# Capped attention and two feed-forward layers in split f32: a 16-bit low-bits step, new planner costs, and one more pair of weight blocks by seven products

## The chip, the core and the metric

The kernel runs on one core of a Trainium2 chip, in one launch. The metric is the device time of that launch in microseconds; less is better. The kernel before took 559.13 us (median of three runs, 558.51 to 560.42).

## The reference: what is computed

```python
scores = cap * tanh((q @ k.T / sqrt(64)) / cap)   # batch 2, 12 heads, 448 rows, 64 wide
attn   = exp(scores - max) / (sum + 1e-9)
x      = (attn @ v) as (896, 768)                  # heads side by side
h = x @ w_in;   g = s * relu(h)**2 + b;   x = g @ w_out          # layer 0: 768 -> 2048 -> 768
h = x @ w_in2;  g = h * clip(h + 3, 0, 6) / 6;  out = g @ w_out2 # layer 1: 768 -> 2048 -> 768
```

All inputs and the output are f32; 896 rows are two batches of 448.

## The kernel before: how it is built and what sets its order

**Stages.** Attention first (to about 88 us), then 18 early pieces of layer 0 interleaved with the end of attention, then the two layers. Everything is kept transposed: features on the 128 partitions, the 448 rows of one batch along the free axis.

**Split products.** A value of the two layers is held as two tiles, an upper part rounded to TensorE's fast f32 form (fp32r) and the rest ("hi" and "lo"). A *piece* is one 128x128 weight block against one 448-column tile and takes three matmuls (L230: hi x lo, lo x hi, hi x hi). `PIECE` in the planner is one of them.

**Weights.** A weight arrives in the raw tile as eight bytes each, the bits of a 64-bit float, and is turned into f32 on the chip by four steps in `convert` (L467): `rescale` on ScalarE (L211) takes the upper word as f32 and shifts its exponent; `low_bits` on ScalarE (L218) takes three bits from the top of the lower word and writes them beside the upper word; `shift` on VectorE (L222) moves the rescaled bits left by three; `merge` on VectorE (L228) joins both with the sign. `parts` (L485) then makes hi (ScalarE cast, L492) and lo (VectorE subtraction, L494), in a weight tile of pool gA or gB, two of each. Input-side blocks are 768 wide, two to a pair; output-side blocks are 512 wide, two to a group of 1024. Three raw tiles are filled by SyncE's DMA queue (L200), each as soon as the merge of its former content is done.

**Products.** 16 blocks `f` of 128 hidden features make a layer's first half. A pair of blocks by the plain way is 24 pieces (two blocks, two batches, six pieces each). By Strassen and Winograd's way (`strassen`, L614) it is seven products P1 to P7 of three pieces, 21 pieces, and needs more of the other engines: four sums of weight parts (L520 to L523), sums T1 to T4 of the two batches' inputs (L651, once per layer) with their hi and lo (L442, L445), copies of PSUM banks (L619, L622) and sums of them (L626, called d1, before P7 and L629, called d2, before P4). The result of each block and batch goes through ScalarE and VectorE: in layer 0 relu (L576), square (L579), hi (L587), lo (L593). Before the change the first `PLAIN` = 8 blocks of layer 0 are plain, four pairs, and the other twelve pairs of the two layers go by seven products. After each half of the blocks come six output groups of 16 pieces (`out_block`, L530), which read the hi and lo of that half's eight blocks.

**Order.** The instruction order of the two layers is made when the program is built, by `Plan` (L52). Every step is a task with an engine, a cost, its predecessors and the tiles it holds. The planner gives each task a due time from TensorE's sequence, then goes through a simulated time in which each engine takes the task that is due first among those whose predecessors ended at least `LAG` ago; TensorE may choose among its next 36 pieces. The order that comes out is written into the engines' queues, and on the chip each engine keeps to its queue. The costs (L411 to L413) thus change only the order.

Of the kernel before, what the change touches and what calls it, by code (L numbers as in the profile page):

```python
# [7 lines left out]
F32 = mybir.dt.float32  # L8
F32R = mybir.dt.float32r
U32 = mybir.dt.uint32  # L10
U8 = mybir.dt.uint8
I32 = mybir.dt.int32
AF = mybir.ActivationFunctionType
ALU = mybir.AluOpType
PSUM = bass.MemoryType.PSUM

B, H, S, D = 2, 12, 448, 64
# [11 lines left out]
WARM = (S, S, S // 4)  # L29
SCALE = 1.0 / D**0.5  # L30
FIRST = 3
PLAIN = 8
SLOTS_A, SLOTS_B = 36, 48
GROUPS = {"gA": 2, "gB": 2}
OUT_ORDER = (0, 3, 1, 4, 2, 5)
# [16 lines left out]
class Plan:  # L52


    LAG = 0.15
    WINDOW = 36

    def __init__(self, sizes):
# [2 lines left out]
    def add(self, engine, cost, run, after=(), use=(), soon=None):  # L61
        t = Task(engine, cost, run, after, list(use), len(self.tasks))
        for u in t.use:
            u.left += 1
        for a in t.after:
            a.then.append(t)
        t.soon = soon
        self.tasks.append(t)
        return t
# [102 lines left out]
def attention_moe_moe(ctx: ExitStack, tc: tile.TileContext, qk, v, cap, w1i, w1o, s, b, w2i, w2o, out):  # L172
    nc = tc.nc
# [6 lines left out]
    st = const.tile([128, 1], F32, name="st")  # L180
# [24 lines left out]
    def rescale(raw, n, bits, dve=False):  # L205
        up = raw_up(raw, n).bitcast(F32)
        up = up.rearrange("p (n m) -> p n m", m=BL) if len(bits.shape) == 3 else up
        if dve:
            nc.vector.tensor_scalar(bits, up, 2.0**-112, None, op0=ALU.mult)
        else:  # L210
            nc.scalar.activation(bits, up, AF.Copy, scale=2.0**-112)  # L211

    def low_bits(raw, n, dve=False):
        by = raw[:, :n, :].rearrange("p m t -> p (m t)").bitcast(U8).rearrange("p (m t) -> p m t", t=8)
        if dve:
            nc.vector.tensor_scalar(by[:, :, 4], by[:, :, 3], 5, None, op0=ALU.logical_shift_right)
        else:
            nc.scalar.activation(by[:, :, 4], by[:, :, 3], AF.Copy, scale=1.0 / 32.0, bias=-15.5 / 32.0)  # L218

    def shift(bits):  # L220
        bits = bits.bitcast(U32)
# [185 lines left out]
    def feed_forward(sb):  # L407
        banks = first_ps + [psum()] + [ps_v.tile([128, 512], F32, name="pav") for _ in range(3)] + [ps_z.tile([128, 512], F32, name="pz")]
        plan = Plan({"slot": 0, "bank": 0, "raw": 0, "gA": 0, "gB": GROUPS["gB"]})
        add = plan.add  # L410
        dve = lambda n, ps=False: 0.15 + 0.00105 * n + (0.06 if ps else 0)  # L411
        dve2 = lambda n: 0.16 + 0.00051 * n
        acts = lambda n, bias=False: 0.19 + 0.00085 * n + (0.08 if bias else 0)  # L413
        PIECE = 0.609
        pools = {"a": [sa, SLOTS_A], "b": [sb, SLOTS_B]}

# [9 lines left out]
        def t_of(r, dt):  # L426
            if r.tile is None:
                where = next(p for p in pools.values() if p[1] > 0)
                where[1] -= 1
                r.home = where  # L430
                r.tile = where[0].tile([128, S], dt, name="sl", tag="s")
            return r.tile
# [4 lines left out]
        def split(src, after, deadline=None, bias=None, psum_src=False, use_src=()):  # L437

            hi, lo = res("slot"), res("slot")

            def upper():
                nc.scalar.copy(t_of(hi, F32R), src())  # L442

            def lower():
                nc.vector.tensor_sub(t_of(lo, F32R), src(), hi.tile.bitcast(F32))  # L445
            a = add("ACT", acts(S), upper, after, [hi, *use_src], deadline)
            c = add("DVE", dve(S, psum_src), lower, [a], [hi, lo, *use_src], deadline)
            return Value(hi, lo, [a, c])

        held = lambda kind, tile: Res(kind, tile)  # L450
# [16 lines left out]
        def convert(src, n, bits, before, blocks, raw=None, stage=0):  # L467

            r = raw or res("raw")

            def tile_of():
                if r.tile is None:
                    r.tile = raw_tile()
                return r.tile
            f = add("DMA", n * 0.0024, lambda: load_raw(tile_of(), src, n), (), [r]) if raw is None else None
            land = add("WAIT", 0, None, ()) if False else f
            a = add("ACT", acts(n), lambda: rescale(r.tile, n, bits), [land, *before], [r]) if stage < 1 else None
            l = add("ACT", acts(n), lambda: low_bits(r.tile, n), [a, land], [r])
            sh = add("DVE", dve2(n), lambda: shift(bits), [a, *before])
            m = add("DVE", dve(n), lambda: merge(r.tile, n, bits), [sh, l], [r])  # L480
            for k in blocks:
                w_users[k] += [t for t in (a, sh, m) if t is not None]
            return m
# [83 lines left out]
        def activation(layer, f, bi, c_psum, made, c_slot=None):  # L567

            src_res = c_psum or c_slot
            src = (lambda: c_psum.tile[:, :S]) if c_psum else (lambda: c_slot.tile)  # L570
            t = c_slot if (c_slot and layer == 0) else res("slot")
            soon = 1.5 if c_psum else 3.0

            def relu():
                o = t.tile if t is c_slot else t_of(t, F32)
                nc.scalar.activation(o, src(), AF.Relu, **({"bias": three} if layer else {}))  # L576
            a = add("ACT", acts(S, layer), relu, made, [src_res, t] if t is not src_res else [t], soon)
            if layer == 0:
                q = add("DVE", dve(S), lambda: nc.vector.scalar_tensor_tensor(out=t.tile, in0=t.tile, scalar=st, in1=t.tile, op0=ALU.mult, op1=ALU.mult), [a], [t])  # L579
            else:  # L580
                q = add("DVE", dve2(S), lambda: nc.vector.tensor_scalar(t.tile, t.tile, 6.0, 1.0 / 6.0, op0=ALU.min, op1=ALU.mult), [a], [t], soon + 1)
                q = add("DVE", dve(S, True), lambda: nc.vector.tensor_mul(t.tile, src(), t.tile), [q], [t, src_res], soon + 2)
            hi, lo = res("slot"), res("slot")

            def upper():
                if layer == 0:
                    nc.scalar.activation(t_of(hi, F32R), t.tile, AF.Identity, bias=bt)  # L587
                else:
                    nc.scalar.copy(t_of(hi, F32R), t.tile)

            def lower():
                if layer == 0:
                    nc.vector.scalar_tensor_tensor(out=t_of(lo, F32R), in0=t.tile, scalar=bt, in1=hi.tile.bitcast(F32), op0=ALU.add, op1=ALU.subtract)  # L593
                else:
                    nc.vector.tensor_sub(t_of(lo, F32R), t.tile, hi.tile.bitcast(F32))
            h = add("ACT", acts(S, layer == 0), upper, [q], [t, hi])
            l = add("DVE", dve(S), lower, [h], [t, hi, lo])
            G[f, bi] = Value(hi, lo, [h, l])

        G = {}  # L600
# [13 lines left out]
        def strassen(layer, f, w, ops):  # L614

            a, bb, c = new_bank(), new_bank(), new_bank()
            p1 = product(w["A11"], ops["B11"], a)
            head = take_pe()
            cp = add("ACT", acts(S), lambda: nc.scalar.copy(bb.tile[:, :S], a.tile[:, :S]), p1, [a, bb])  # L619
            p5 = product(w["S1"], ops["T1"], c)  # L620
            s5 = res("slot")
            c5 = add("ACT", acts(S), lambda: nc.scalar.copy(t_of(s5, F32), c.tile[:, :S]), p5, [c, s5])  # L622
            p2 = product(w["A12"], ops["B21"], a, [cp], first=False)
            p6 = product(w["S2"], ops["T2"], bb, [cp], first=False, seeded=True)
            mid = take_pe()
            d1 = add("DVE", dve(S, True), lambda: nc.vector.tensor_add(c.tile[:, :S], bb.tile[:, :S], s5.tile), [*p6, c5], [bb, c, s5], 0.5)  # L626
            p7 = product(w["S3"], ops["T3"], bb, [d1], first=False, seeded=True)
            s7 = res("slot")
            d2 = add("DVE", dve(S, True), lambda: nc.vector.tensor_add(t_of(s7, F32), bb.tile[:, :S], s5.tile), [*p7], [bb, s5, s7], 0.5)  # L629
            p3 = product(w["S4"], ops["B22"], c, [d1], first=False)  # L630
            p4 = product(w["A22"], ops["T4"], bb, [d2], first=False, seeded=True)
            tail = take_pe()
            activation(layer, f, 0, a, p2)
            activation(layer, f, 1, c, p3)
            activation(layer, f + 1, 1, None, [d2], s7)
            activation(layer, f + 1, 0, bb, p4)
            return head, mid, tail
# [47 lines left out]
        for layer in range(2):  # L685
            partial = {}
            for half in range(2):
# [5 lines left out]
                for mt in OUT_ORDER:  # L693
# [3 lines left out]
                    for bi in range(B):  # L697
                        before = []
                        if half:
                            p, t = partial[mt, bi]  # L700
                            before = [add("ACT", acts(S), lambda p=p, q=bank[bi]: nc.scalar.copy(q.tile[:, :S], p.tile), [t], [p, bank[bi]])]
                        made.append(product(w, [G[half * HF + k, bi] for k in range(HF)], bank[bi], before, seeded=bool(half)))
                        pe.extend(take_pe())
                    if half == 0:
                        for bi in range(B):
                            p = res("slot")
                            t = add("ACT", acts(S), lambda p=p, q=bank[bi]: nc.scalar.copy(t_of(p, F32), q.tile[:, :S]), made[bi], [p, bank[bi]], 1.0)
# [180 lines left out]
```

## Time and profile before

| | |
|---|---|
| median of three runs | 559.13 us |
| the profiled execution's own time | 558.14 us |
| its span, first to last instruction | 556.4 us |
| TensorE busy | 543.7 us, 98% |
| ScalarE (ACT) busy | 423.6 us, 76% |
| VectorE (DVE) busy | 394.4 us, 71% |
| DMA engines busy | 34% |
| granted TensorE clock | full in every slice of the span |

A matmul's busy time in the profile (about 367 ns) is longer than the distance to the next one, since matmuls are pipelined. So TensorE's pace is read from the distance of starts, and a pause from a start that comes later than that distance. Likewise the next instruction on VectorE or ScalarE starts before the recorded end of the one before.

### The profile page before, as it was taken

What the parts mean: (1) busy time and instruction counts of PE and PEld (TensorE: products, weight loads), DVE (VectorE), ACT (ScalarE), POOL (GpSimd) and SP (SyncE); (2) the same over time, 40 slices, a digit from 0 to 9 for tenths busy, and PEclk for the clock granted to TensorE, in tenths of its full rate; (3) what the DMA queues carried; (4) which work ended last, traced back from release to release, by engine and by line L of the source; (5) the groups of instructions that cost most, each with busy time, mean ns of one, the idle gap of its engine ahead of it and who ended that gap; (6) DMA issues with size and microseconds to landing.
All of it is one profiled execution on the core that took longest, in us unless ns stands there. A gap on an engine that the chain in (4) does not pass through costs nothing.

```text
span 556.4 us, 7002 instructions
## 1 busy us (share of the span) xinstructions
PE 543.7 (98%) x2682; PEld 438.4 (79%) x2682; DVE 394.4 (71%) x587; ACT 423.6 (76%) x549; POOL 0.4 (0%) x5
## 2 busy tenths in 40 slices
PE   8999999999979999999999999999999999999997
PEld 3322234789969998889999999989999888889996
DVE  2689887878988506898866898899554688994400
ACT  6999993399997518899999758985875788888701
POOL 0000000000000000000000000000000000000000
PEclk9999999999999999999999999999999999999999
DMA  8833411042354503222444322212453322125211
GB/s 314 326 107 111 154 53 41 0 152 90 139 151 137 184 1 114 94 77 77 125 147 163 121 107 94 77 65 84 147 197 133 114 94 77 59 98 180 105 51 49
DMA packets 16860, 64.13 MB, mean 115 GB/s; under 512 B 2214, under 2 KB 4154, under 8 KB 16698
## 3 DMA queue, kind: packets, MB, share of 16 engines
q1 hardware_dynamic: 16680, 63.52, 33.8%
q8 instruction: 21, 0.34, 0.2%
q10 hardware_dynamic: 146, 0.16, 0.1%
q14 instruction: 13, 0.11, 0.1%
HBM read 60.88 MB, written 2.79 MB: 114 GB/s over the span
## 4 chain that ended last, share of the span: by engine, by line
PE 71%; ACT 16%; DVE 9%; issue 3%
PE pf L232 31%; PE pav L232 20%; PE pz L232 7%; ACT raw L218 7%; PE ps L265 5%; PE pav L291 4%; ACT w L211 3%; DVE gBl L494 2%; DVE w L228 2%; ACT t L273 2%; ACT gAh L492 1%; PE pav L288 1%; DVE sl L579 1%; ACT t L278 1%; DVE sl L593 1%
## 5 line engine op out<-in xcount | busy, mean ns | idle before, releaser
L232 PE MATMUL pf<-sl,gBh 128*128 128x448 f32 x450 | 128.5, 367 | 0.4 <-DVE sl L593 0.4
L218 ACT ACTIVATE raw<-raw 128x512 uint8<-128x512 uint8 (+1 forms) x77 | 116.9, 1607 | 0.3
L228 DVE SCALAR_TENSOR_TENSOR w<-raw,w 128x512 uint32<-128x512 uint32 (+1 forms) x80 | 63.6, 798 | 46.3 <-ACT raw L218 46.2
L232 PEld LDWEIGHTS pf<-sl,gBh 128*128 128x128 f32 x450 | 84.4, 188 | 8.0 <-DVE sl L593 0.7
L232 PE MATMUL pf<-sl,gBl 128*128 128x448 f32 x225 | 83.0, 369 | 4.9 <-ACT sl L587 2.8
L232 PE MATMUL pav<-sl,gBh 128*128 128x448 f32 x238 | 68.0, 367 | 0.0
L211 ACT ACTIVATE w<-raw 128x512 f32<-128x512 f32 (+1 forms) x79 | 57.9, 763 | 7.6 <-DVE gBl L494 5.4
L232 PE MATMUL pf<-sl,gAh 128*128 128x448 f32 x198 | 56.6, 367 | 0.0
L494 DVE TENSOR_TENSOR gBl<-w,gBh 128x1024 fp32r<-128x1024 f32 (+1 forms) x29 | 37.0, 1277 | 26.5 <-ACT gBh L492 26.4
L232 PEld LDWEIGHTS pf<-sl,gBl 128*128 128x128 f32 x225 | 42.3, 188 | 10.5 <-ACT sl L587 3.1
L232 PE MATMUL pav<-sl,gAh 128*128 128x448 f32 x172 | 49.0, 366 | 0.0
L232 PEld LDWEIGHTS pav<-sl,gBh 128*128 128x128 f32 x238 | 44.7, 188 | 4.0
L222 DVE TENSOR_SCALAR w<-w 128x512 uint32<-128x512 uint32 (+1 forms) x80 | 37.2, 476 | 12.3 <-ACT w L211 11.9
L492 ACT CAST gBh<-w 128x1024 fp32r<-128x1024 f32 (+1 forms) x29 | 31.9, 1100 | 18.3 <-PE pf L232 6.1
L232 PE MATMUL pav<-sl,gBl 128*128 128x448 f32 x119 | 43.8, 368 | 0.0
L273 ACT ACTIVATE t<-ps 128x896 f32<-128x896 f32 x42 | 37.9, 902 | 6.5 <-PE ps L265 6.5
L278 ACT ACTIVATE t<-t 128x896 f32<-128x896 f32 x42 | 39.9, 949 | 1.2
L232 PEld LDWEIGHTS pf<-sl,gAh 128*128 128x128 f32 x198 | 37.2, 188 | 3.4
L494 DVE TENSOR_TENSOR gAl<-w,gAh 128x1536 fp32r<-128x1536 f32 (+2 forms) x24 | 34.3, 1432 | 6.9 <-ACT gAh L492 6.8
L492 ACT CAST gAh<-w 128x1536 fp32r<-128x1536 f32 (+2 forms) x24 | 29.2, 1219 | 13.0 <-DVE w L521 11.4
L232 PE MATMUL pf<-sl,gAl 128*128 128x448 f32 x99 | 36.3, 367 | 0.0
L265 PE MATMUL ps<-rqk 64*128 64x448 f32 x144 | 34.7, 585 | 0.5 <-ACT t L273 0.5
(157 smaller groups left out, 931.4 us busy)
## 6 DMA issues: line engine op xcount, KB each, us to landing
raw<-in_w1i SPq DMA_DIRECT2D x16, 768.0 KB, 4.3
raw<-in_w1o SPq DMA_DIRECT2D x24, 512.0 KB, 3.4
raw<-in_w2i SPq DMA_DIRECT2D x16, 768.0 KB, 4.3
raw<-in_w2o SPq DMA_DIRECT2D x24, 512.0 KB, 3.5
rqk<-in_qk SPq DMA_DIRECT2D x11, 448.0 KB, 5.8
out<-sl SPq DMA_DIRECT2D x12, 224.0 KB, 1.9
rb<-rows SPq DMA_DIRECT2D x10, 224.0 KB, 3.7
va<-in_v SPq DMA_DIRECT2D x1, 1344.0 KB
```

Source lines behind the costliest of these rows:

```text
L211: nc.scalar.activation(bits, up, AF.Copy, scale=2.0**-112)
L218: nc.scalar.activation(by[:, :, 4], by[:, :, 3], AF.Copy, scale=1.0 / 32.0, bias=-15.5 / 32.0)
L222: nc.vector.tensor_scalar(bits, bits, 3, None, op0=ALU.logical_shift_left)
L228: nc.vector.scalar_tensor_tensor(out=bits, in0=up, scalar=0x80000007, in1=bits, op0=ALU.bitwise_and, op1=ALU.bitwise_or)
L232: nc.tensor.matmul(ps[:, :S], w[a], rhs[r], start=start and i == 0, stop=stop and i == 2, skip_group_check=True)
L265: nc.tensor.matmul(ps[:, j, :S], raw_qk[p][rows, 1, c * 128:(c + 1) * 128], raw_qk[p][rows, 0, :], start=True, stop=True)
L273: nc.scalar.activation(u_t[n], u_ps.pop(n)[:, :, :S], AF.Tanh, scale=icap_r)
L278: nc.scalar.activation(u_t[n], u_t[n], AF.Exp, scale=cap_r)
L288: nc.tensor.matmul(pav[p + o][(top, end)[j], :S], va[bi][keys, d, 4 * NC + col, :], u_t[n][keys, col, :], start=o == 1, stop=o == 0)
L291: nc.tensor.matmul(pav[p][(top, end)[j], :S], va[bi][:, d, (2 * (p % 2) + j) * NC + c, :], u_t[n][:, j, :], start=(p % 2 == 0 and c == 0), ...
L492: nc.scalar.copy(g.tile[0][:, at:at + n], cols)
L494: c = add("DVE", dve(n), lambda: nc.vector.tensor_sub(g.tile[1][:, at:at + n], cols, g.tile[0][:, at:at + n].bitcast(F32)), [a], [g])
```

## The change

Three edits. `low_bits` reads and writes the same place through 16-bit instead of 8-bit elements: on ScalarE it multiplies the 16-bit word that holds the wanted bits by 2^-13 where it multiplied the byte by 2^-5. The planner gets other costs and a longer `LAG`. And `PLAIN` goes from 8 to 6, so that the fourth pair of layer 0 (f = 6 and 7) goes by seven products, which puts the T sums of layer 0 before the first group of output pieces and not behind it.

```diff
-PLAIN = 8
+PLAIN = 6
...
-    LAG = 0.15
+    LAG = 0.25
...
     def low_bits(raw, n, dve=False):
-        by = raw[:, :n, :].rearrange("p m t -> p (m t)").bitcast(U8).rearrange("p (m t) -> p m t", t=8)
+        by = raw[:, :n, :].rearrange("p m t -> p (m t)").bitcast(U16).rearrange("p (m t) -> p m t", t=4)
         if dve:
-            nc.vector.tensor_scalar(by[:, :, 4], by[:, :, 3], 5, None, op0=ALU.logical_shift_right)
+            nc.vector.tensor_scalar(by[:, :, 2], by[:, :, 1], 13, None, op0=ALU.logical_shift_right)
         else:
-            nc.scalar.activation(by[:, :, 4], by[:, :, 3], AF.Copy, scale=1.0 / 32.0, bias=-15.5 / 32.0)
+            nc.scalar.activation(by[:, :, 2], by[:, :, 1], AF.Copy, scale=2.0**-13, bias=0.5**14 - 0.5)
...
-        dve = lambda n, ps=False: 0.15 + 0.00105 * n + (0.06 if ps else 0)
-        dve2 = lambda n: 0.16 + 0.00051 * n
-        acts = lambda n, bias=False: 0.19 + 0.00085 * n + (0.08 if bias else 0)
+        dve = lambda n, scalar=False: 0.075 + 0.00104 * n + (0.06 if scalar else 0)
+        dve2 = lambda n: 0.07 + 0.00052 * n
+        acts = lambda n, scaled=False: 0.09 + (0.00093 if scaled else 0.00084) * n + (0.055 if scaled else 0)
...
-            a = add("ACT", acts(n), lambda: rescale(r.tile, n, bits), [land, *before], [r]) if stage < 1 else None
-            l = add("ACT", acts(n), lambda: low_bits(r.tile, n), [a, land], [r])
+            a = add("ACT", acts(n, True), lambda: rescale(r.tile, n, bits), [land, *before], [r]) if stage < 1 else None
+            l = add("ACT", acts(n, True), lambda: low_bits(r.tile, n), [a, land], [r])
```

The other changed lines only say which cost a VectorE step is given.

TensorE, around the fourth pair of layer 0, as it was: the last pieces of block 7 (batch 1, bank pz_830; xh and xl are the hi and lo of the attention's result), then at once the first output group with block 0, 1 and so on (sl tiles), all eight blocks of batch 0 in bank pf_726.

```order
L232 MATMUL pz_830<-xh15_94,gAl_1018 128x448
L232 MATMUL pz_830<-xl15_95,gAh_1017 128x448
L232 MATMUL pz_830<-xh15_94,gAh_1017 128x448
L232 MATMUL pf_726<-sl_920,gBl_1096 128x448
L232 MATMUL pf_726<-sl_936,gBh_1095 128x448
L232 MATMUL pf_726<-sl_920,gBh_1095 128x448
L232 MATMUL pf_726<-sl_926,gBl_1096 128x448
```

The same place now: the last matmul of P1 (bank pav_827), P5 (pav_828), P2 (pav_827), P6 (pav_829), then three output pieces in pz_830, then P7 (pav_829 again, behind d1), P3 and P4.

```order
L232 MATMUL pav_827<-xh02_76,gAh_1037 128x448
L232 MATMUL pav_828<-sl_903,gAl_1038 128x448
...
L232 MATMUL pav_827<-xh03_78,gAl_1038 128x448
...
L232 MATMUL pav_829<-sl_937,gAl_1038 128x448
...
L232 MATMUL pz_830<-sl_1130,gBl_1110 128x448
L232 MATMUL pz_830<-sl_1157,gBh_1109 128x448
...
L232 MATMUL pav_829<-sl_998,gBl_1019 128x448
L232 MATMUL pav_829<-sl_1043,gBh_1018 128x448
...
L232 MATMUL pav_828<-xh13_90,gBl_1019 128x448
...
L232 MATMUL pav_829<-sl_1088,gBl_1019 128x448
L232 MATMUL pav_829<-sl_1115,gBh_1018 128x448
```

24 pieces became 21, and three output pieces stand between P6 and P7.

VectorE, from the end of attention on (behind the last lo of the attention's result), as it was: squares (L579) come between the steps of block 3's weights.

```order
L222 TENSOR_SCALAR w<-w 128x768
L651 TENSOR_TENSOR sl<-xf 128x448
L579 SCALAR_TENSOR_TENSOR sl<-sl,st 128x448 x3
L228 SCALAR_TENSOR_TENSOR w<-raw,w 128x768
L222 TENSOR_SCALAR w<-w 128x768
L228 SCALAR_TENSOR_TENSOR w<-raw,w 128x768
L579 SCALAR_TENSOR_TENSOR sl<-sl,st 128x448
L494 TENSOR_TENSOR gAl<-w,gAh 128x768
```

And now, from the same instruction on: sums of inputs come first, and the first square, which was the second instruction behind that L222, is now the 43rd, behind nearly all the T sums.

```order
L222 TENSOR_SCALAR w<-w 128x768
L651 TENSOR_TENSOR sl<-xf 128x448 x3
L651 TENSOR_TENSOR sl<-xf,sl 128x448
L228 SCALAR_TENSOR_TENSOR w<-raw,w 128x768
L222 TENSOR_SCALAR w<-w 128x768
L651 TENSOR_TENSOR sl<-xf,sl 128x448
L228 SCALAR_TENSOR_TENSOR w<-raw,w 128x768
...
L651 TENSOR_TENSOR sl<-xf,sl 128x448
L445 TENSOR_TENSOR sl<-sl 128x448
L579 SCALAR_TENSOR_TENSOR sl<-sl,st 128x448
L445 TENSOR_TENSOR sl<-sl 128x448
```

Twelve sums and twelve lo parts (L651, L445) thus moved ahead of the 16 squares and 16 lo parts of the first eight blocks' results.

## Rows read from the trace of the kernel before

**Rows 1.** The page: shares of the chain that ended last, by line.
```profile
PE pf L232 31%; PE pav L232 20%; PE pz L232 7%; ACT raw L218 7%; PE ps L265 5%; PE pav L291 4%; ACT w L211 3%; DVE gBl L494 2%; DVE w L228 2%; ACT t L273 2%; ACT gAh L492 1%; PE pav L288 1%; DVE sl L579 1%; ACT t L278 1%; DVE sl L593 1%
```

**Rows 2.** Timeline, TensorE, first output group: start, length, instruction, idle before and releaser.
```profile
153.88 0.36 PE L232 MATMUL pf<-sl,gBl 128*128 128x448 f32 x1
...
157.73 0.57 PE L232 MATMUL pf<-sl,gBh 128*128 128x448 f32 x2
161.05 0.48 PE L232 MATMUL pf<-sl,gBl 128*128 128x448 f32 x1 [2.75 <-ACT sl L587]
161.98 0.67 PE L232 MATMUL pf<-sl,gBh 128*128 128x448 f32 x2 [0.45 <-DVE sl L593]
162.49 0.36 PE L232 MATMUL pf<-sl,gBl 128*128 128x448 f32 x1
```

**Rows 3.** Timeline, TensorE: two other pauses, each behind the matmul before it.
```profile
116.67 0.37 PE L232 MATMUL pav<-xh,gAh 128*128 128x448 f32 x1
117.29 0.47 PE L232 MATMUL pav<-xh,gAl 128*128 128x448 f32 x1 [0.26 <-DVE gAl L494]
...
485.66 0.56 PE L232 MATMUL pf<-sl,gAh 128*128 128x448 f32 x2
487.34 0.47 PE L232 MATMUL pf<-sl,gBl 128*128 128x448 f32 x1 [1.12 <-DVE pz L626]
```

**Rows 4.** Chain of waits in order of time: start, length, merged instructions.
```profile
177.24 14.60 PE pav L232 x72
...
288.63 14.88 PE pav L232 x72
...
537.83 14.89 PE pf L232 x72
```

**Rows 5.** ScalarE by line and form: count, busy us, mean ns, idle before.
```profile
L218 ACT ACTIVATE raw<-raw 128x512 uint8<-128x512 uint8 x48 | 62.1, 1388 | 0.2
L218 ACT ACTIVATE raw<-raw 128x768 uint8<-128x768 uint8 x29 | 54.8, 1971 | 0.1
...
L211 ACT ACTIVATE w<-raw 128x512 f32<-128x512 f32 x48 | 30.9, 672 | 2.0 <-DMA raw<-in_w2o 1.0 <-DMA raw<-in_w1o 0.9
L211 ACT ACTIVATE w<-raw 128x768 f32<-128x768 f32 x31 | 27.0, 905 | 5.5 <-DVE gBl L494 5.4
```

**Rows 6.** Waits, all engines: us in total, times, longest.
```profile
DVE w L228 <- ACT raw L218: 46.2, 61, 3.4
```

**Rows 7.** Timeline, VectorE, behind the attention's end.
```profile
108.17 0.56 DVE L222 TENSOR_SCALAR w<-w 128x768 uint32<-128x768 uint32 x1
...
128.99 0.68 DVE L579 SCALAR_TENSOR_TENSOR sl<-sl,st 128x448 f32<-128x448 f32 x1
129.59 2.46 DVE L593 SCALAR_TENSOR_TENSOR sl<-sl,bt 128x448 fp32r<-128x448 f32 x4
```

**Rows 8.** Timeline, VectorE, before the TensorE pause at 466.5 us.
```profile
463.20 0.96 DVE L228 SCALAR_TENSOR_TENSOR w<-raw,w 128x768 uint32<-128x768 uint32 x1 [1.18 <-ACT raw L218]
464.96 0.96 DVE L228 SCALAR_TENSOR_TENSOR w<-raw,w 128x768 uint32<-128x768 uint32 x1 [0.80 <-ACT raw L218]
465.83 0.62 DVE L629 TENSOR_TENSOR sl<-pf,sl 128x448 f32<-128x448 f32 x1
```

**Rows 9.** VectorE by line and form, as group 5.
```profile
L228 DVE SCALAR_TENSOR_TENSOR w<-raw,w 128x768 uint32<-128x768 uint32 x32 | 30.7, 958 | 24.1 <-ACT raw L218 24.1
L579 DVE SCALAR_TENSOR_TENSOR sl<-sl,st 128x448 f32<-128x448 f32 x32 | 21.3, 680 | 0.2 <-ACT sl L576 0.2
L494 DVE TENSOR_TENSOR gAl<-w,gAh 128x1536 fp32r<-128x1536 f32 x12 | 21.0, 1753 | 2.5 <-ACT gAh L492 2.5
L494 DVE TENSOR_TENSOR gBl<-w,gBh 128x1024 fp32r<-128x1024 f32 x17 | 20.8, 1223 | 6.3 <-ACT gBh L492 6.3
...
L445 DVE TENSOR_TENSOR sl<-sl 128x448 fp32r<-128x448 f32 x24 | 14.7, 620 | 0.3
...
L222 DVE TENSOR_SCALAR w<-w 128x768 uint32<-128x768 uint32 x32 | 17.7, 557 | 7.8 <-ACT w L211 7.8
```

More of the change, by code (lines that the diff above doesn't have):

```diff
@@ L10 @@
 U32 = mybir.dt.uint32
-U8 = mybir.dt.uint8
+U16 = mybir.dt.uint16
 I32 = mybir.dt.int32
@@ L446, in split @@
             a = add("ACT", acts(S), upper, after, [hi, *use_src], deadline)
-            c = add("DVE", dve(S, psum_src), lower, [a], [hi, lo, *use_src], deadline)
+            c = add("DVE", dve(S), lower, [a], [hi, lo, *use_src], deadline)
             return Value(hi, lo, [a, c])
@@ L578, in activation @@
             if layer == 0:
-                q = add("DVE", dve(S), lambda: nc.vector.scalar_tensor_tensor(out=t.tile, in0=t.tile, scalar=st, in1=t.tile, op0=ALU.mult, op1=ALU.mult), [a], [t])
+                q = add("DVE", dve(S, True), lambda: nc.vector.scalar_tensor_tensor(out=t.tile, in0=t.tile, scalar=st, in1=t.tile, op0=ALU.mult, op1=ALU.mult), [a], [t])
             else:
                 q = add("DVE", dve2(S), lambda: nc.vector.tensor_scalar(t.tile, t.tile, 6.0, 1.0 / 6.0, op0=ALU.min, op1=ALU.mult), [a], [t], soon + 1)
-                q = add("DVE", dve(S, True), lambda: nc.vector.tensor_mul(t.tile, src(), t.tile), [q], [t, src_res], soon + 2)
+                q = add("DVE", dve(S), lambda: nc.vector.tensor_mul(t.tile, src(), t.tile), [q], [t, src_res], soon + 2)
             hi, lo = res("slot"), res("slot")
@@ L596, in activation @@
             h = add("ACT", acts(S, layer == 0), upper, [q], [t, hi])
-            l = add("DVE", dve(S), lower, [h], [t, hi, lo])
+            l = add("DVE", dve(S, layer == 0), lower, [h], [t, hi, lo])
             G[f, bi] = Value(hi, lo, [h, l])
@@ L625, in strassen @@
             mid = take_pe()
-            d1 = add("DVE", dve(S, True), lambda: nc.vector.tensor_add(c.tile[:, :S], bb.tile[:, :S], s5.tile), [*p6, c5], [bb, c, s5], 0.5)
+            d1 = add("DVE", dve(S), lambda: nc.vector.tensor_add(c.tile[:, :S], bb.tile[:, :S], s5.tile), [*p6, c5], [bb, c, s5], 0.5)
             p7 = product(w["S3"], ops["T3"], bb, [d1], first=False, seeded=True)
             s7 = res("slot")
-            d2 = add("DVE", dve(S, True), lambda: nc.vector.tensor_add(t_of(s7, F32), bb.tile[:, :S], s5.tile), [*p7], [bb, s5, s7], 0.5)
+            d2 = add("DVE", dve(S), lambda: nc.vector.tensor_add(t_of(s7, F32), bb.tile[:, :S], s5.tile), [*p7], [bb, s5, s7], 0.5)
             p3 = product(w["S4"], ops["B22"], c, [d1], first=False)
```

## The prediction, made before the changed kernel was run

> **What bounds the kernel now.** I first read the page's chain by line: TensorE's matmuls of the two layers (L232) hold 58% of the span, and the one step that stands out beside them is ScalarE's L218, the low bits, with 7%, some 38 us [rows 1]. Then TensorE's timeline from 88 us on, looking for starts that come later than the pace. The pace has two values in this trace, both at full granted clock: 72 matmuls in 14.60 us are 0.2028 us each, 72 in 14.88 us are 0.2067 us [rows 4]. TensorE changes from one to the other at pauses, with no cause that I can see; 242 to 355 us and 487 us to the end run slow, most of the rest fast.
>
> The pauses are few. The largest is in the first output group: two matmuls start at 157.73 and should end their turn at 158.14; the next starts at 161.05, then 161.98, and the two after it take 0.51 instead of 0.41 [rows 2]. Beyond the pace that is 2.91 + 0.73 + 0.10 = 3.7 us, released by ScalarE's L587 and VectorE's L593, the hi and lo of the last plain block. At 117.29 there is one of 0.42 us and 0.11 at its restart, released by L494 [rows 3]. Behind 162 us eight more of 0.2 to 1.4 us each make 4.7 us in all; the last and longest begins behind 485.66 and ends at 487.34, 1.28 us late and 0.11 at the restart, released by L626 [rows 3]. So 9.0 us of pauses could go; the rest of the two layers is TensorE's own work.
>
> Who is late in them is a mixture of ScalarE and VectorE. VectorE waits 46.2 us in 61 places for L218 [rows 6]. Shortly before the pause at 466.5 us its two merges wait 1.18 and 0.80 us for L218, and L629, which TensorE waits for there, stands behind them in the queue [rows 8].
>
> **The nine matmuls.** 24 pieces become 21: 9 matmuls of 0.2028 us, **-1.8 us**, if nothing new makes TensorE wait.
>
> **The 16-bit step.** No row shows a 16-bit operation on ScalarE. The byte form costs 1.97 us for 768 columns and 1.39 for 512; `rescale`, the same function on the same stride of eight bytes in f32, 0.905 and 0.672 [rows 5]. The f32 row is the lower bound that I use, though the step could undercut it a little; the byte rows are the upper, though two bytes could cost more than one. The 16-bit form resembles the byte form in that it writes part of a word in place, and the f32 form in that nothing is narrower than a half word. I take the f32 price, because the byte form's extra is per element (1.07 us over 768, 0.72 over 512, about 1.4 ns each in both), which looks like the handling of a byte operand and not like a fixed cost of writing in place; this is the weakest choice here. By it ScalarE loses 29 x 1.07 + 48 x 0.72 = 65 us of its 424 busy. All but what lies in the pauses is hidden beside TensorE.
>
> The Trainium skill ("ScalarE: Activation LUTs", What ACT_TABLE_LOAD costs) gives one element a cycle at 1.2 GHz for f32 and bf16 alike, 186 ns and 0.833 ns per element. By it a 768-wide step would take 826 ns, an estimate from that page, near the f32 row's 905; the byte row is far from it, and the page says nothing on bytes.
>
> **The first pair by seven products.** In the old trace the first output group starts at 153.88 [rows 2]. The 24 pieces of blocks 6 and 7 before it are 72 x 0.2028 = 14.6 us, so block 6 starts at 139.3. The pause at 117.29 goes: VectorE's L494 stands behind a merge that ScalarE's L218 releases a microsecond sooner. That is **-0.5 us**, and P1 starts at 138.8. P1, P5, P2, P6 and the three output pieces are 15 pieces, 45 matmuls, 9.1 us: TensorE wants P7, and with it d1 (L626), at 147.9.
>
> VectorE has now more to do before d1. Its queue from the L222 at 108.17 [rows 7] holds, up to d1: 5 L222 and 5 L228 of 768, 2 and 2 of 512, 12 L651, 12 L445, lo parts of 768 (three), 1024, 1152 and 1536, four weight sums of 384, 11 squares, 7 lo parts of results, d1. Starts follow at the mean length less 0.08 us (0.60 for the L579 at 128.99, whose mean is 0.680 [rows 7, 9]). So: 5 x 0.48 + 5 x 0.88 = 6.8; the 512-wide ones 2 x 0.34 + 2 x 0.61 = 1.9; L651, L445 and d1, of one size and form of operation, 25 x 0.54 = 13.5; lo parts at 1.14 for 1024, 1.67 for 1536, and by their slope of 1.04 ns per element 1.28 for 1152 and 0.88 for 768, together 6.7; weight sums by the same slope 4 x 0.48 = 1.9; 18 x 0.60 = 10.8 for squares and lo parts, which are also scalar_tensor_tensor of 448. Sum 41.6 us, and about 0.8 us of waits for ScalarE's first merges that are left at the f32 price. d1 is done at 150.6, 2.7 us after TensorE wants it. The copy L619 before P2 stands in ScalarE's queue behind L587s that follow VectorE's squares, so part of these 2.7 us may show one product earlier; the sum is the same.
>
> From there to the last lo that the first group needs it is 10 us more on VectorE, and TensorE has nine pieces of products and seven output pieces, 9.7 us, before it asks for that one: no second pause. So 3.7 us of pause become 2.7: **-1.0 us**. At the byte price each of the five wide merges is held up to 0.9 us longer, and d1 comes some 3.7 us later.
>
> **Later pauses.** Eight, 4.7 us. Before each stand L218 steps of the same pair, two of them worth 2.1 us by rows 5, more than any of these pauses. What does not shorten is VectorE's own work, and two of the longest pauses (2.4 us of the 4.7) are waits for L626 in a queue that is nearly full. I take 1.5 us left, **-3.2 us**, with 0 and 6 as bounds. The planner's new costs and `LAG` act here and nowhere else; they set the order by distances that the rows confirm for VectorE (0.075 + 0.06 + 0.00104 x 448 = 0.60, the L579 distance), and I give them no term of their own.
>
> Attention up to 88 us keeps its order on TensorE; its three low-bits steps on VectorE end nothing there. SyncE's loads keep their order in the weights: each waits for a merge, and the merges come sooner. The tail is the same last product and output.
>
> **Sum.** -1.8 - 0.5 - 1.0 - 3.2 = -6.5 us on the profiled execution's 558.14, that is 551.6 us. The median of the runs before is 1.0 us above that execution, so I predict **552.6 us**. Pace: 188 us of the old trace run at 0.2067. All fast would take off 188 x 2% = 3.6 us more; all slow would add some 5.2 us. I keep the old mixture, and its chance is the largest part of the range. The forecast's own range is 548.5 to 556.5.
>
> **Rivals.**
> *The 16-bit form costs as the byte did (slower).* The Trainium skill ("SBUF — State Buffer", Door 1: The DMA port swizzle) says that an access which crosses into a new 16-byte line pays, so that only a stride of a few elements is free. Here, as a mechanism of this kernel: f32, 16-bit and byte steps all go by eight bytes, the f32 row reads so at 0.9 ns per element [rows 5] and writes packed, so it would be the strided write that costs, and 16 bits leave it. Then the place is d1: 2.7 + 3.7 = 6.4 us of pause instead of 3.7 (+2.7). Further on, both versions of the planner charge L218 less than it costs (0.843 then, 0.859 now), but the old one hid that by charging other ScalarE steps too much: 0.571 for a 448-wide copy that it now charges 0.466. Ten such steps in each of 13 pairs are 13.7 us of allowance gone; the old order was short by 27 us on the 24 wide steps and 36 us on the 48 narrow ones and paid 8.4 us, 13%; so 13% of 13.7, +1.8 us. With -1.8 and nothing else: 558.14 + 2.7 + 1.8 - 1.8 = 560.8, on the median's scale **561.8**. Between -6.5 at 0.905 us and +2.7 at 1.97 the point from which it is slower is about 1.66 us for 768 columns. For it: the partial write. Against it: the per-element extra of the byte.
> *VectorE, not ScalarE, is what is late.* Then the later pauses stay and only the products and the 0.5 us remain, with the first pause as before: 558.14 - 2.3 + 1.0 = **556.8**. For it: two waits are for L626, and VectorE's load in the first stretch. Against it: 46.2 us of VectorE's waits for L218.
> *The pace falls to 0.2067 throughout:* 552.6 + 5.2 = **557.8**. For it: the last 65 us did. Against it: of the pauses most were followed by the fast pace.
>
> **How the numbers follow.** Forecast 0.66, byte price 0.13, VectorE 0.16, slow pace 0.05. A measurement can tell 0.3%, 1.7 us: faster is under 557.45, slower over 560.8. Faster: 0.65 of the forecast, 0.09 of VectorE's case, 0.74 in all; same 0.18, from VectorE's, the pace's and half of the byte's case; slower 0.08, the other part of the byte's. The range is 547.5 to 560: under it lie the fast pace with all pauses gone, over it most of the byte price.
>
> **What would show it.** L218 at 768 columns near 0.9 us and VectorE's wait for it under 20 us in all; nine matmuls fewer; a pause at P7 or P2 near 139 to 151 us of about 2.7 us; no pause in the first output group; behind it few pauses, 1.5 us together; and the share of 0.2067. An L218 above 1.6 us, a first pause over 6 us or more than 5 us of later pauses would make the prediction wrong.

## The result, and the profile after

The changed kernel took 564.43 us (median of six runs, 563.67 to 565.97) against 558.82 us of the kernel before beside it: ratio 1.0102, interval 1.0079 to 1.0125. It is slower by 1%, where 552.6 us and a range of 547.5 to 560 had been forecast. Of e2 below, one execution of six ran at a granted clock of 0.56 from end to end, took 885.09 us and is left out.

The profiled execution took 565.01 us, 6.9 more than that of before. ScalarE by line and form, as [rows 5]:

```profile
L218 ACT ACTIVATE raw<-raw 128x512 uint16<-128x512 uint16 x48 | 62.7, 1383 | 0.1
L218 ACT ACTIVATE raw<-raw 128x768 uint16<-128x768 uint16 x29 | 54.7, 1980 | 0.1
...
L211 ACT ACTIVATE w<-raw 128x512 f32<-128x512 f32 x48 | 31.1, 672 | 4.6 <-DMA raw<-in_w2o 3.2 <-DVE gAl L494 0.9 <-DMA raw<-in_w1o 0.2
L211 ACT ACTIVATE w<-raw 128x768 f32<-128x768 f32 x31 | 27.1, 906 | 4.0 <-DVE gBl L494 2.5 <-DVE gAl L494 1.4
```

The 16-bit form takes 1.980 and 1.383 us where the byte form took 1.971 and 1.388. Nothing was saved. VectorE's wait for it is down only from 46.2 us [rows 6] to 41.5. That wait, and what TensorE waited for in the layers, by line (us in total, times, longest):

```profile
DVE w L228 <- ACT raw L218: 41.5, 52, 1.7
...
PE pav L232 <- ACT pav L619: 6.8, 1, 6.8
PE pz L232 <- DVE sl L629: 1.9, 2, 1.3
PE pav L232 <- DVE pav L626: 1.6, 3, 0.9
```

The 6.8 us are at the fourth pair: P2 waits for the copy L619. TensorE's timeline there, the last two matmuls of P5 first:

```profile
141.63 0.57 PE L232 MATMUL pav<-sl,gAh 128*128 128x448 f32 x2
148.97 0.74 PE L232 MATMUL pav<-xh,gAl 128*128 128x448 f32 x1 [6.77 <-ACT pav L619]
149.51 0.57 PE L232 MATMUL pav<-xl,gAh 128*128 128x448 f32 x1
149.88 0.58 PE L232 MATMUL pav<-xh,gAh 128*128 128x448 f32 x1
...
152.12 0.44 PE L232 MATMUL pav<-xh,gAh 128*128 128x448 f32 x1
152.40 0.37 PE L232 MATMUL pav<-sl,gAl 128*128 128x448 f32 x1
```

P2 should start at 142.04 and starts at 148.97. Its matmuls then follow at 0.37 us, not at 0.20: the granted clock is about half. The next two lines are stretches: from and to, length, then busy time and count of each engine (PE, weight loads, VectorE, ScalarE, POOL), and behind POOL the granted clock:

```profile
148.90:152.50 3.60, 3.53 (x10) 3.17 (x11) 3.40 (x7) 3.36 (x6) 0.00 (x0) 0.53 0.02 5
152.50:160.00 7.50, 7.50 (x38) 6.82 (x37) 7.19 (x14) 4.70 (x8) 0.00 (x0) 1.00 0.00 0
```

0.53 for those 3.6 us, nearly the lower level of 1.2 GHz, then full: some 1.6 us more. What stood before L619 on ScalarE:

```profile
145.04 0.67 ACT L587 ACTIVATE sl<-sl,bt 128x448 fp32r<-128x448 f32 x1 [1.09 <-DVE sl L579]
145.62 0.66 ACT L211 ACTIVATE w<-raw 128x512 f32<-128x512 f32 x1
...
147.16 1.33 ACT L218 ACTIVATE raw<-raw 128x512 uint16<-128x512 uint16 x1
148.23 0.69 ACT L619 COPY pav<-pav 128x448 f32<-128x448 f32 x1
```

P1's last matmul had started at 140.01, so L619's input was there some eight microseconds before it ran. L619 stood behind L587 steps that waited for VectorE's squares, and behind a conversion. The first square (the 45th instruction behind the L222 in this trace, not the 43rd) is late itself: it starts at 140.87, where e1 below, the same order with a cheap step, has it at 136.29. All five wide merges before it waited for L218, 0.39 to 1.06 us each, 3.6 us together:

```profile
117.78 0.96 DVE L228 SCALAR_TENSOR_TENSOR w<-raw,w 128x768 uint32<-128x768 uint32 x1 [1.06 <-ACT raw L218]
...
127.08 0.96 DVE L228 SCALAR_TENSOR_TENSOR w<-raw,w 128x768 uint32<-128x768 uint32 x1 [0.79 <-ACT raw L218]
...
140.87 0.68 DVE L579 SCALAR_TENSOR_TENSOR sl<-sl,st 128x448 f32<-128x448 f32 x1
```

**Where the 6.9 us came from**, by distances of TensorE's starts. The first pair with its restart and the low clock costs 8.5 us, where the first output group had cost 3.7 [rows 2]: +4.8. The pause at 117 is gone: -0.5. Pauses behind the first output group make 9.7 us instead of 4.7: +5.1. Nine matmuls: -1.8. Together +7.6; some 0.5 us less up to the end of attention, and a little less of the slow pace (some 170 us for 184), make up the rest.

### The profile page after: what moved, and what is told of

It reads as the page before. It is cut to its first block, busy times and chain, and to the rows that moved or that the text cites. A ratio compares the mean times of both kernels' runs of the same rounds, so it can differ in the third digit from the quotient of the medians.

```text
span 563.2 us, 7021 instructions
## 1 busy us (share of the span) xinstructions
PE 544.4 (97%) x2673; PEld 437.1 (78%) x2673; DVE 398.1 (71%) x593; ACT 425.0 (75%) x551; POOL 0.4 (0%) x5
## 5 line engine op out<-in xcount | busy, mean ns | idle before, releaser
L218 ACT ACTIVATE raw<-raw 128x512 uint16<-128x512 uint16 (+1 forms) x77 | 117.4, 1608 | 0.1
L232 PE MATMUL pf<-sl,gBh 128*128 128x448 f32 x358 | 102.2, 367 | 0.0
L228 DVE SCALAR_TENSOR_TENSOR w<-raw,w 128x512 uint32<-128x512 uint32 (+1 forms) x80 | 63.5, 797 | 41.9 <-ACT raw L218 41.5
L232 PEld LDWEIGHTS pf<-sl,gBh 128*128 128x128 f32 x358 | 67.3, 188 | 5.9
L232 PE MATMUL pf<-sl,gAh 128*128 128x448 f32 x246 | 70.3, 367 | 0.0
L232 PE MATMUL pav<-sl,gAh 128*128 128x448 f32 x244 | 69.6, 366 | 0.0
L232 PE MATMUL pf<-sl,gBl 128*128 128x448 f32 x179 | 66.0, 369 | 0.7 <-DVE sl L629 0.6
L232 PEld LDWEIGHTS pav<-sl,gAh 128*128 128x128 f32 x244 | 45.9, 188 | 4.0
L494 DVE TENSOR_TENSOR gBl<-w,gBh 128x1152 fp32r<-128x1152 f32 (+1 forms) x26 | 33.5, 1288 | 20.5 <-ACT gBh L492 20.4
L492 ACT CAST gBh<-w 128x1152 fp32r<-128x1152 f32 (+1 forms) x26 | 28.8, 1106 | 24.2 <-DVE w L523 8.7
L222 DVE TENSOR_SCALAR w<-w 128x512 uint32<-128x512 uint32 (+1 forms) x80 | 37.0, 475 | 12.4 <-ACT w L211 11.9
L232 PE MATMUL pav<-sl,gAl 128*128 128x448 f32 x122 | 44.7, 366 | 0.0
```

Of the source, the lines that this page charges most:

```text
L218: nc.scalar.activation(by[:, :, 2], by[:, :, 1], AF.Copy, scale=2.0**-13, bias=0.5**14 - 0.5)
L222: nc.vector.tensor_scalar(bits, bits, 3, None, op0=ALU.logical_shift_left)
L228: nc.vector.scalar_tensor_tensor(out=bits, in0=up, scalar=0x80000007, in1=bits, op0=ALU.bitwise_and, op1=ALU.bitwise_or)
L232: nc.tensor.matmul(ps[:, :S], w[a], rhs[r], start=start and i == 0, stop=stop and i == 2, skip_group_check=True)
L492: nc.scalar.copy(g.tile[0][:, at:at + n], cols)
L494: c = add("DVE", dve(n), lambda: nc.vector.tensor_sub(g.tile[1][:, at:at + n], cols, g.tile[0][:, at:at + n].bitcast(F32)), [a], [g])
```

## The experiments

Each is a small edit of the changed kernel or of the one before; times are medians, ratios are to the kernel before on the same chip.

| | edit | us | ratio, interval |
|---|---|---|---|
| changed kernel | | 564.43 | 1.0102, 1.0079 to 1.0125 |
| e1 | low bits on 3/8 of the columns | 549.89 | 0.9855, 0.9807 to 0.9903 |
| e2 | byte form | 563.68 | 1.0095, 1.0064 to 1.0126 |
| e3 | fourth pair plain | 566.35 | 1.0144, 1.0104 to 1.0183 |
| e4 | true price | 553.72 | 0.9894, 0.9845 to 0.9943 |
| e5 | true price, fourth pair plain | 548.80 | 0.9840, 0.9795 to 0.9885 |
| e6 | before, fourth pair by seven | 557.98 | 0.9989, 0.9963 to 1.0015 |
| e9 | before, true price | 553.18 | 0.9908, 0.9876 to 0.9940 |
| e11 | LAG 0.15 | 566.63 | 1.0161, 1.0111 to 1.0210 |
| e12 | old charges, LAG 0.25 | 556.22 | 0.9977, 0.9951 to 1.0003 |
| v2, seven | whole words | 554.93 | 0.9951, 0.9929 to 0.9973 |
| v2, plain | whole words, fourth pair plain | 552.92 | 0.9918, 0.9889 to 0.9947 |

**e1: the same order with a step that costs what I had assumed.**

```diff
-nc.scalar.activation(by[:, :, 2], by[:, :, 1], AF.Copy, ...)
+nc.scalar.activation(by[:, :n * 3 // 8, 2], by[:, :n * 3 // 8, 1], AF.Copy, ...)
```

> The changed kernel with its own order on every engine, but the low-bits step on ScalarE treats only the first 3/8 of the columns (the other weights keep the rescaled word without their last three bits). The step should then take about 0.88 us at 768 and 0.66 us at 512, the f32 price that I had taken. Theory A (the price of the 16-bit step is what was mis-sized, the rest of the forecast holds): the 6.9 us pause at the first pair by seven products falls to about 2.7 us, time 551 to 555 us. Theory B (VectorE's load and the new order lose the time, whatever the step costs): the pause stays above 5 us, time 560 us or more.

549.89 us. ScalarE's rows, and TensorE's two waits in the layers that are over 0.3 us:

```profile
L218 ACT ACTIVATE raw<-raw 128x192 uint16<-128x192 uint16 x48 | 27.8, 656 | 0.1
L218 ACT ACTIVATE raw<-raw 128x288 uint16<-128x288 uint16 x29 | 23.0, 885 | 0.1
```
```profile
PE pav L232 <- ACT pav L619: 2.1, 1, 2.1
...
PE pav L232 <- DVE pav L626: 0.9, 1, 0.9
```

VectorE's first square there:

```profile
136.29 0.68 DVE L579 SCALAR_TENSOR_TENSOR sl<-sl,st 128x448 f32<-128x448 f32 x1
```

At 0.885 and 0.656 us the pause at the first pair is 2.3 us by distance of starts, at P2 (2.7 forecast, for P7 or P2), the later pauses make 1.9 us (1.5 forecast), and VectorE waits 6.1 us for L218 in all. Two things stand beside that: behind the pause the clock falls and costs 1.6 us, and this execution kept the fast pace, for which the forecast's number is 549. So the time lies under the 551 to 555 us that I expected of e1, in part by the luck of the pace; two of its four executions took 551 to 552. Theory A's mechanism holds, B falls: VectorE's load by itself costs about what the prediction had said.

**e2: the byte form in the new order.**

```diff
-bitcast(U16) ... by[:, :, 2], by[:, :, 1], scale=2.0**-13, bias=0.5**14 - 0.5
+bitcast(U8)  ... by[:, :, 4], by[:, :, 3], scale=1.0 / 32.0, bias=-15.5 / 32.0
```

> The changed kernel with the old byte form of the step and everything else as changed. Theory A (16 bits cost as the byte did): the same time as the changed kernel within 0.3%, 563 to 566 us, L218 at 1.97 and 1.39 us. Theory B (same): no difference. Theory C (the 16-bit form is worth something that the means hide): over 567 us.

563.68 us, the changed kernel's time within the intervals. The two forms are worth the same; that edit does nothing. No row of e2's profile is used.

**e3 and e6: the fourth pair alone.** `PLAIN = 8` in the changed kernel, `PLAIN = 6` in the one before.

> The changed kernel with the fourth pair of layer 0 plain again (24 pieces). Theory A: the order made for a cheap step still loses, but without the pile of work before the first seven products: 558 to 562 us, no pause above 4 us. Theory B: the loss is all in the place of the fourth pair: 556 to 558 us, the old time or less.

> The kernel before with its byte step, costs and LAG, only the fourth pair of layer 0 by seven products. Theory A (the new costs lose the time, the pair gains): 555 to 560 us, nine matmuls fewer against some pause at the first seven products. Theory B (the pair's place loses the time): 562 us or more with a pause above 5 us.

566.35 and 557.98 us. Both theories for e3 missed: the plain pair does not help. It has nine matmuls more, 1.8 us, and its median is 1.9 us above the changed kernel's, though the intervals overlap. The pause is then at the old place and longer (2.75 us in [rows 2]):

```profile
PE pf L232 <- ACT sl L587: 3.9, 1, 3.9
```

In e6 the pair's pause at L619 is 3.4 us, with a stretch of low clock behind it. By distance of starts e6 has 3.6 us more of pauses and low clock than the kernel before; the nine matmuls give 1.8 us back and a larger share of the fast pace the rest: no difference to be measured. So the place of the pair is not the loss, in either order. Nor is it a gain that can be counted on: in the traces of the changed kernel, e1, e4, e6, e11 and e12, whatever the charges, the low clock behind the pause at L619 costs some 1.4 to 1.6 us, nearly all that the nine matmuls save.

**e4, e5, e9: tell the planner the price.**

```diff
-l = add("ACT", acts(n, True), lambda: low_bits(r.tile, n), [a, land], [r])
+l = add("ACT", 0.00227 * n - 0.04, lambda: low_bits(r.tile, n), [a, land], [r])
```

> The changed kernel with the planner told what the step takes by the trace (start to start 1.70 us at 768, 1.12 at 512) and nothing else. Theory A: the planner puts the copy L619 ahead of the conversions that hold it, the 6.9 us pause and the loss of clock behind it go: 553 to 558 us. Theory B: VectorE's work before d1 is the same, so the first pause stays above 4 us and the time above 560 us.

> The changed kernel with the true price of the low-bits step in the planner and the fourth pair of layer 0 plain again. Theory A: the price alone repairs the order; against the run with the price and the fourth pair by seven products this one has nine matmuls more (1.8 us) and no pause at the first L619: 553 to 557 us, under the kernel before. Theory B (the pair's place decides): 557 us or more, or clearly under 552.

> The kernel before with only the price of the low-bits step in its planner set to what the trace shows (1.70 and 1.12 us), its other charges too high as they were. Theory A: the pause of 3.7 us in the first output group goes, later ones shrink: 553 to 557 us. Theory C (the old surcharges had already made up for the price, so that pricing it twice changes little): 557 to 560 us.

553.72, 548.80 and 553.18 us: all three are under the kernel before. e9 is the plainest case: one charge set right in the old kernel, and between 107 and 338 us no start on its TensorE comes late by 0.05 us or more; the 3.7 us of the first output group [rows 2] are gone. In e4 the step still takes 1.988 us at 768, and TensorE waits 2.1 us for L619, with some 1.6 us of low clock behind it, so the loss of clock did not go as I had expected:

```profile
139.30 1.38 ACT L218 ACTIVATE raw<-raw 128x512 uint16<-128x512 uint16 x1
...
142.78 0.54 ACT L576 ACTIVATE sl<-pf 128x448 f32<-128x448 f32 x1 [0.58 <-DVE sl L593]
...
144.15 0.54 ACT L619 COPY pav<-pav 128x448 f32<-128x448 f32 x1
```

The narrow conversions are now done at 140.7; L619 then stands behind other steps of ScalarE, one of which waits 0.58 us for VectorE. e5 is the fastest kernel of the study that computes everything; its largest pause in the layers is 0.7 us:

```profile
PE pav L232 <- DVE pf L626: 0.7, 1, 0.7
```

For e5 I had expected 553 to 557 us; 548.80 is what its Theory B, that the pair's place decides, allowed with "clearly under 552". But B is not shown either. e5 has nine matmuls more than e4 and yet a smaller median: in the profiles, from 105 us to the end of the first pair, e4 has 4.6 us of pause and low clock, 3.9 of them at that pair, and e5 has 1.2; and e4 ran at 0.2067 us per matmul for some 285 us while e5 ran nearly all at 0.203, which is more than 5 us of the difference. The intervals overlap, so which way is better is not shown.

**e11 and e12: LAG or charges.** `LAG = 0.15` in the changed kernel; or its LAG with the charges of before:

```diff
-acts = lambda n, scaled=False: 0.09 + (0.00093 if scaled else 0.00084) * n + (0.055 if scaled else 0)
+acts = lambda n, scaled=False: 0.19 + 0.00085 * n + (0.08 if scaled and n == S else 0)
```
and likewise `dve` and `dve2`.

> The changed kernel with the old LAG of 0.15 and the new costs. Theory A (the new, lower charges for the other steps took away the allowance that had covered the low-bits step): no better than the changed kernel, 562 to 570 us. Theory L (the longer LAG is what spoilt the order): 556 to 560 us.

> The changed kernel with LAG 0.25 and the old charges for VectorE's and ScalarE's steps (the surcharge for PSUM sources left out), the low-bits step charged 0.84 and 0.63 us. Theory A: the old surcharges cover part of the low-bits step again: 555 to 560 us, like the old kernel with the fourth pair by seven products (558). Theory L: 562 us or more.

566.63 and 556.22 us. LAG is not it. The new, lower charges are: with the old ones the order is again as good as before, though L218 was charged as wrongly (0.843 us at 768). e12 puts back ScalarE's and VectorE's charges together, so which engine's covered L218 is not shown.

**The forms of the step, one look.** In turn: as it is (L223); written packed to a tile of its own (L225); 16 bits read, f32 words written on the stride (L227); f32 words read and written on the stride (L229).

> One look at prices, not at the time. The kernel with the true price, but the low-bits step takes four forms in turn: as it is (16 bits read and written in place on a stride of eight bytes), 16 bits read on the stride and written packed to a tile of their own, 16 bits read and full f32 words written on the stride, f32 words read and written on the stride; the last three leave the last three bits of the weights wrong or missing. Theory P (a part of a word written costs): the first 1.97 us at 768, also the second, the last two about 0.9. Theory S (a strided write costs, whatever its width): the second about 0.9, the other three near 1.97. Theory R (reading a part of a word costs): the first three near 1.97, the last 0.9.

```profile
L223 ACT ACTIVATE raw<-raw 128x768 uint16<-128x768 uint16 x8 | 15.6, 1955 | 0.0
L227 ACT ACTIVATE raw<-raw 128x512 f32<-128x512 uint16 x12 | 8.2, 683 | 0.0
...
L227 ACT ACTIVATE raw<-raw 128x768 f32<-128x768 uint16 x7 | 6.4, 912 | 0.0
L229 ACT ACTIVATE raw<-raw 128x768 f32<-128x768 f32 x7 | 6.4, 910 | 0.0
L225 ACT ACTIVATE scratch<-raw 128x768 uint16<-128x768 uint16 x7 | 6.3, 900 | 0.0
```

None of the three theories as written: reading half a word costs nothing extra (0.912 against 0.910 us), nor does writing whole words on the stride (0.912), nor writing half words side by side (0.900). Only half words written on the stride of eight bytes take 1.955 us.

**v2: whole words.** ScalarE writes the three bits as a 32-bit word over the lower word, VectorE takes it up in the shift:

```diff
+nc.scalar.activation(raw[:, :n, 0], by[:, :, 1], AF.Copy, scale=2.0**-13, bias=0.5**14 - 0.5)
-nc.vector.tensor_scalar(bits, bits, 3, None, op0=ALU.logical_shift_left)
+nc.vector.scalar_tensor_tensor(out=bits, in0=bits, scalar=3, in1=low, op0=ALU.logical_shift_left, op1=ALU.bitwise_or)
```

> A version that writes whole words: ScalarE reads the 16-bit word on the stride and writes the three bits as a full 32-bit word over the lower word; VectorE joins them in the shift (two sources, so 0.88 instead of 0.47 us start to start at 768), the merge keeps the sign alone. The planner has these prices; the fourth pair goes by seven products. Theory P (a part of a word written on a stride is what costs): L218's successor takes about 0.91 and 0.68 us, ScalarE loses some 60 us of busy time, VectorE gains 25; time 545 to 551 us. Rival (VectorE becomes the bound of the runs of seven products): 553 us or more with pauses released by L626 and L629.

> As the version before it, with the fourth pair of layer 0 plain. Theory P: 546 to 551 us, about 1.8 us above the one by seven products if TensorE's pace is alike, less if that one pauses at its first L619. Rival: as above, 553 us or more.

554.93 and 552.92 us: under the kernel before, but not the 545 to 551 that I expected. The step is cheap (rows of the plain version), and in the plain version the pauses behind 200 us are above all two for d1 (L636 here):

```profile
L222 ACT ACTIVATE raw<-raw 128x512 uint32<-128x512 uint16 x48 | 30.6, 668 | 0.0
L222 ACT ACTIVATE raw<-raw 128x768 uint32<-128x768 uint16 x29 | 25.2, 905 | 0.0
```
```profile
PE pav L242 <- DVE pf L636: 3.6, 2, 1.8
```

55 us of ScalarE's work went (368.2 busy against 423.6), VectorE got the 20 us of the second source (414.5 busy against 394.4), and d1 is late. In the plain version the clock falls behind each of the two pauses (0.57 from 469.5 to 473.5 us), some 1.6 us more each. Of the version by seven products the rival has time and cause right (3.4 us of waits for L636); the plain one has the cause, with a time between the two expectations. e5 stays the best version.

## Why the prediction was wrong

- **The step that failed is the price of the 16-bit step.** "I take the f32 price, because the byte form's extra is per element": 0.905 and 0.672 us were assumed, 1.980 and 1.383 measured. The extra is per element and is still not due to the byte: it belongs to each part of a word written on the stride (the forms above). A cost per element does not tell operand from destination; I read it as if it did. The choice was named the weakest, and the chance of 0.13 for its upper bound was too low: the form nearest to the new one, in place, on the same stride, in parts of a word, was the byte's.
- **The rest of the sum holds, to within some 2 us, once that price is given.** e1 has my price and the same order: 549.89 us, in the forecast's own range (548.5 to 556.5); first pause 2.3 for 2.7, later ones 1.9 for 1.5, nine matmuls fewer, no pause at 117. The prediction had no term for the low clock behind the first pause (1.6 us), and the fast pace more than made up for it: that much of the agreement is luck.
- **The rival "costs as the byte did" was the case, and too small:** 561.8 for 564.4. Its place was right (6.4 us of pause, 6.9 measured, at L619 and not at d1), but it had no low clock behind a pause (1.6 us), and +1.8 us for the later pauses where +5.1 were measured. (Its 63 us of shortfall were taken from recorded lengths; by the distances of starts that e4 charges, 1.70 and 1.12 us, they are 44, and +1.8 becomes +2.6, still too small.) Its cause for the later pauses is borne out by e11 and e12: the old charges for other steps had covered L218, the new ones no longer did. That it was ScalarE's charges alone, as the rival had it, is not shown.
- **"I give them no term of their own"**, of the planner's costs, was wrong with the price that came: they are what separates 564 from 556 (e12). That L218 was charged half its time in both planners (0.84 and 0.86 us, where starts follow at 1.70) stood in the rows and in the diff; the gain was in correcting that (e4, e5, e9), not in the step.
- **VectorE as what is late:** not by itself in the changed kernel, where L218 holds VectorE's merges; true in v2, once ScalarE is relieved.
- **Pace:** the mixture stayed, and so did its size. The forecast's term was right, its cause is not known.
- The Trainium skill ("SBUF — State Buffer", Door 1: The DMA port swizzle) gives strides of 4 fp32, 8 bf16 or 16 int8 elements as free. The stride here is eight bytes, two f32, four 16-bit or eight byte elements, so that page gave no reason for the rival that was put beside it. For whole words the trace agrees: f32 read and written on that stride take 0.910 us, the f32 step that writes packed 0.905. For half words it does not: 1.955 us on the stride, 0.900 packed.
- The 826 ns estimated from "ScalarE: Activation LUTs" (What ACT_TABLE_LOAD costs) of the Trainium skill are near the 0.9 us of whole words and far from partial ones, on which that section says nothing.

What stays open: why a part of a word written on the stride costs more; what sets TensorE's pace after a pause; and whether the fourth pair by seven products gains anything under the true price.

## What to carry to other kernels

Where a planner sets the order, compare each of its charges with the traced distance of starts before any of them is changed: two wrong charges can cover each other, and correcting one uncovers the other. In these runs a strided write of half words on ScalarE costs more than twice the same write in whole words (1.955 against 0.912 us); look at the destination first, not at the width of the operand. Take the price of an unseen form from the nearest row in how it writes, or measure all forms in one run.

## What the runs showed of the hardware that was not expected

- Partial words written on a stride by ScalarE: 1.955 to 1.992 us for 768 columns in 16 bits, 1.971 in bytes [rows 5]; 0.900 packed, 0.912 as f32 words on the stride, 0.905 as 32-bit words.
- Short pauses can be followed by a stretch at about half the clock (matmuls 0.37 us apart): 3.4 us of it after the 6.9 us pause, and in e1 about as much behind a pause of only 2.3 us (granted clock 0.57 from 144 to 148 us). Length alone does not tell: in v2's plain version it follows pauses of 2.0 and 1.9 us, while the 2.9 and 0.7 us of the kernel before [rows 2] and the pauses of 2.0, 1.9 and 1.9 us in v2 by seven products had none (granted clock 1.00 behind each).

```profile
144.00:148.00 4.00, 4.00 (x14) 3.56 (x13) 4.00 (x7) 3.42 (x8) 0.00 (x0) 0.57 0.02 4
```

- Two paces at full granted clock, 0.203 and 0.2067 us per matmul [rows 4]. Most traces here mix them; those of e1, e5 and v2's plain version run nearly all at the fast one. With some 450 us of such matmuls the mixture can move a time by up to 9 us (an estimate: 450 x 2%), more than most edits of this study.
